# Chunks 1 and 2 of the first layer by seven products per block, in a kernel with a written-out order

## The chip, the cores and the metric

The kernel runs on 1 core of one Trainium2 chip. The metric is the device time of one execution in microseconds (us). The kernel before takes 623.67 us, the median of 3 runs (623.22 to 624.69).

## The reference

Eight batches of 576 tokens with 8 heads of 64 go through a linear attention, and its result through a feed-forward layer whose hidden value is the largest of three products.

```python
q_s = exp(q - max(q, -1)); q_s /= sum(q_s, -1) + 1e-9
k_s = exp(k - max(k, 2));  k_s /= sum(k_s, 2) + 1e-9
x   = q_s @ (k_s^T @ v)                # per batch and head, then 4608 x 512
h   = max(x @ w1, x @ w2, x @ w3)      # w1, w2, w3: 512 x 768
out = h @ w_out                        # 768 x 512, fp32
```

## The kernel before, in words

**Number format.** An operand of the layer is held as two fp32r words, a high one (a cast) and a low one (the value less its cast). A product of two operands is three matmuls, high by low, low by high and high by high. One matmul is 128x128 by 128x512.

**Weights.** The four matrices arrive as pairs of 32-bit words in twelve slices: 0 to 8 are (jp, i), two of the six hidden column blocks of one of w1, w2, w3; 9 to 11 are `w_out`. `Slices.join` rebuilds the fp32 value on VectorE (L535 or ScalarE's L533, then L537, L538, L542); GpSimd adds the low word in two halves (L548, the word sums); ScalarE casts the high word (L556) and VectorE subtracts for the low word (L562, `lo`, whose end is called split). `keep` stores the fp32 value to DRAM (L569). Chunk 0's second product reads `w_out`'s slices 9, 10, 11 in that order of its rows.

**Chunks.** The tokens are nine chunks of 512: rows 0 to 511 of each batch are chunks 0 to 7, and the last 64 rows of all eight batches (the left queries, `left_queries`, L940) are chunk 8. Chunks 0, 1 and 2 are plain: 18 gate groups of 12 matmuls (L1004), the maximum of three (L1017), the split of the hidden value (L1021, L1024), and four second products of 18 matmuls (L1051). A group named (j, i) belongs to block u = 3*(j // 2) + i, so a block is two groups of one chunk. Chunks 3 to 8 are three `Duo`s: two chunks together by Winograd's scheme, per block u of nine seven products P1 to P7 (L1237), six matmuls each, where plain ones would be eight; then seven products for the second layer (L1415). The scheme needs sums of operands: of x (`convert`, L1176 to L1182), of the hidden value (`operands`, L1346 to L1352), and of weights (`mix_weights`, L1086: load, four additions on 128x256 at L1113, a cast, two low words at L1119, store). Its weights are then loaded per product from DRAM (`keep_a`, `keep_s`).

**Attention.** A `Pair` n is two heads of a batch, four pairs to a batch. Batches 0 and 1 (n 0 to 7) have row softmax work in 64 columns; from batch 2 on two pairs share a query tile: load (L660), maximum (L822), 18 exponentials on ScalarE (L826), sums and quotient (L841 to L845), a 32x32 transpose (L850, into `tb`), then small DMAs from `tb` into `qT` (L865), and x by TensorE (L920). The query tile (`qt2`) lies over the slices' staging buffers `wx`. It may be loaded after `clear`: all slices split (`turn`) and those of `wx` stored. There is one such tile, so each load waits for the use before it. Keys from batch 2 on are maximised over partitions by GpSimd (L726); `open_reducer` (L1511) runs that operation once on a dummy first.

**Order.** Each piece of work is a generator of `Step`s (engine, cost, what it waits for). `ORDER`, a list of generator numbers, is written out: word by word it says which generator issues its next step, and a letter behind the number picks the engine where there is a choice. So every engine works in an order fixed in the text, and one engine never passes a step that waits. SyncE issues all data DMAs, in its order too. Costs and ranks in the code made the list; at run time they decide nothing but the fill products (`products_for_nothing`), matmuls put where TensorE was thought idle.

Of the kernel before, what the change touches and what calls it, by code (L numbers as in the profile page):

```python
# [8 lines left out]
F32 = mybir.dt.float32  # L9
# [14 lines left out]

SIGNAL = 0.26
# [32 lines left out]

X_BY_PE = (1, 2, 3, 6)
# [9 lines left out]
2 117 117V 5 124 0 116 3 20 7 124V 117 117 117 124 124 20A 116G 117V 124 27 21 20 20 124V 4 118 118A 27A 28 116 123  # L69
123 116 123 8 130 130 1 116 20 123A 27 9 20 19 137 10 137 131 116 116A 22 131V 27 130 131 6 123 123 12 142 145 138  # L70
130A 119 119 27 27 123A 141 144 144 131 125 125A 119 23V 137 11 29 130 131 130 137A 144 144A 26 126 24 131V 316 130V
317 143 132 144 126 138 132A 138 30V 25 33 126 35 35V 144 126 35 318 133 13 41 133 138 138V 35 137 137 137V 36 145 145
317 316 139 139V 133 144V 35 133 31 35 32 148 43 318 319 319 43A 151 140 318 140 145 145V 34 317 146 151 37 43 43 140
49 140 319 44 151 151A 156 38V 159 43 316 316 149 152 150 334 318 334 43 14 51 51A 42 52 317 146V 320 51 335 320 151
57 151 45 151A 51 59 46V 320 320 59A 155 334 334 162 39 40 65 165 321 51 165 321 321 59 319 335 322 51 50 59 55 334V
322 322 60 67 53 54V 56 73 75 67A 67 165 321 152 152 322 323 323 336 164 59 335 165A 335 157 323 158 158 147 324 324
323 152 81 324 337 324 325 59 325 63 61 152V 67 62V 64 325 325 68 147 67 147 153 165 153A 165 326 336 75A 165A 326 326
67 337 158 326 83 327 327 327 327 75 69 158A 158 159V 47 75 154 76 163 70V 337 75 159 159 159 83A 328 328 71 329 328
48 329 75 77 328 74 329 329 166 79 336 336 97 159V 160 83 78V 83 330 99 158 158V 84 169 83 83 82 154 154 166 166 166
330 330 331 160A 331 335V 85 161 331 330 166V 86V 87 15 72 161 331 161 336V 167 338 99A 99 99 161 339 332 339 332 100  # L80
332 333 333 332 337 99 167V 333 338 338 89 91 168 99 346 314 91A 91 91 103 168 347 101 92 346 91 333 98 168 339 337
338 348 348 348 348 338 349 91 102V 104 93 105 107 108 94V 107V 346 107 346 107 364 347 347 347 365 349 364 349 107
107 109 342 342 349 365 110V 16 18 343 339 339 314 177 343 343 343 178 342 342 314 95 344 344 345 111 341 344 344 345
# [65 lines left out]
""".split()  # L149


# [38 lines left out]
class Streams:  # L190
# [20 lines left out]
    def ready(self, s, engine):  # L211
# [26 lines left out]
        if engine in step.port:  # L238
            t = max(t, self.port)
# [1437 lines left out]
```

## Time and profile before

| | us |
|---|---|
| median of 3 runs | 623.67 |
| profiled execution | 624.85 |
| its span | 623.1 |
| TensorE busy | 612.0 |
| VectorE busy | 447.4 |
| ScalarE busy | 332.5 |
| GpSimd busy | 49.8 |

The profiled execution is 1.75 us longer than its span, and 1.18 us over the median of the runs. The granted clock was 0.999 of full speed. All times of rows are from the start of the span.

### The profile page before, as it was taken

The numbers are of one execution on the slowest core, as the hardware profiler recorded it, in microseconds if no ns is written. First come the engines' busy times: TensorE is split into PE (matmuls) and PEld (weight loads), VectorE is DVE, ScalarE is ACT, GpSimd is POOL, SyncE is SP. The second block draws the span as 40 slices with busy tenths as digits, with TensorE's granted clock in tenths as the row PEclk, the third lists the DMA queues.
The fourth block names the chain that finished last, engine by engine and source line by source line (L and its number), as shares of the span: only waits on it lengthen the run. The fifth ranks groups of instructions, "written<-read, shape, count | busy, mean of one in ns | idle before, by whom it ended". The sixth has DMA issues, their size and how long they took to land.

```text
span 623.1 us, 9728 instructions
## 1 busy us (share of the span) xinstructions
PE 612.0 (98%) x3383; PEld 493.1 (79%) x3383; DVE 447.4 (72%) x668; ACT 332.5 (53%) x847; POOL 49.8 (8%) x44
## 2 busy tenths in 40 slices
PE   6899999999999999999999999999999999999997
PEld 6677778888777777887787878888887788888886
DVE  7999998468877898969476998453778862344573
ACT  5997873366566667763646566232334832223262
POOL 2234333101000100000000000000000000000000
PEclk9999999999999999999999999999999999999999
DMA  8968488589988778988999977687765546666534
GB/s 310 407 245 313 164 259 301 209 309 329 302 301 290 228 246 248 328 308 275 293 315 276 313 202 232 188 250 245 217 199 150 168 140 196 213 209 196 165 99 144
DMA packets 66256, 152.39 MB, mean 245 GB/s; under 512 B 7584, under 2 KB 18464, under 8 KB 62368
## 3 DMA queue, kind: packets, MB, share of 16 engines
q1 hardware_dynamic: 66064, 151.71, 74.4%
q8 instruction: 27, 0.44, 0.3%
q14 instruction: 21, 0.17, 0.1%
q10 hardware_dynamic: 144, 0.07, 0.0%
HBM read 106.92 MB, written 37.75 MB: 232 GB/s over the span
## 4 chain that ended last, share of the span: by engine, by line
PE 96%; DVE 1%; DMA 1%; ACT 1%; issue 0%; SPq 0%; ACTq 0%
PE pf L1237 41%; PE pf L1004 24%; PE pf L1415 14%; PE pf L1051 8%; PE pa L748 3%; PE pa L920 2%; DMA wst<-in_w_dram 1%; PE pa L892 1%; PE sm L773 0%; PE pa L877 0%; PE pa L695 0%; DVE km L671 0%; DVE wx L537 0%; PE pa L977 0%; PE pf L773 0%
## 5 line engine op out<-in xcount | busy, mean ns | idle before, releaser
L1237 PE MATMUL pf<-xb,ws 128*128 128x512 f32 x1134 | 260.3, 390 | 0.0
L1237 PEld LDWEIGHTS pf<-xb,ws 128*128 128x128 f32 x1134 | 212.4, 188 | 44.4
L1004 PE MATMUL pf<-x,wa 128*128 128x512 f32 x648 | 157.6, 397 | 0.0
L1004 PEld LDWEIGHTS pf<-x,wa 128*128 128x128 f32 x648 | 120.0, 188 | 28.1 <-issue 2.1
L1267 DVE TENSOR_TENSOR mm<-pf,mm 128x512 f32<-128x512 f32 x36 | 24.7, 686 | 66.6 <-PE pf L1237 66.6
L826 ACT ACTIVATE qt<-qt,qm 128x64 f32<-128x64 f32 x180 | 60.1, 336 | 10.3 <-DVE rk L755 6.5
L1287 ACT COPY pf<-pf 128x512 f32<-128x512 f32 x27 | 15.5, 575 | 82.4 <-PE pf L1237 73.0
L548 POOL TENSOR_TENSOR wx<-wx,wst 128x512 int32<-128x512 int32 x24 | 34.5, 1458 | 60.1 <-ACT wst L552 21.2
L726 POOL PARTITION_ALL_REDUCE kma<-km x12 | 13.5, 1123 | 313.8 <-DVE km L723 259.9
L1280 ACT COPY u<-pf 128x512 f32<-128x512 f32 x27 | 15.8, 587 | 38.4 <-PE pf L1237 36.2
L826 ACT ACTIVATION_READ_ACCUMULATOR qt<-qt,qm 128x1 f32 x180 | 33.8, 188 | 0.0
L1017 DVE TENSOR_TENSOR m<-pf,m 128x512 f32<-128x512 f32 x36 | 24.4, 684 | 9.7 <-PE pf L1004 8.7
L1051 PE MATMUL pf<-ol,h_h 128*128 128x512 f32 x72 | 28.5, 396 | 0.0
L1113 DVE TENSOR_TENSOR bdf<-bdf 128x256 f32<-128x256 f32 x48 | 20.3, 422 | 11.3 <-DMA bdf<-keep_w 6.4
L1051 PE MATMUL pf<-oh,h_l 128*128 128x512 f32 x72 | 28.1, 390 | 0.0
L1051 PE MATMUL pf<-oh,h_h 128*128 128x512 f32 x72 | 28.0, 389 | 0.0
L1178 DVE TENSOR_TENSOR xb<-xf,xb 128x1024 fp32r<-128x1024 f32 x18 | 21.9, 1221 | 5.5 <-ACT xb L1176 5.4
L1415 PE MATMUL pf<-mix,so 128*128 128x512 f32 x84 | 25.0, 397 | 0.0
L1280 ACT COPY s<-pf 128x512 f32<-128x512 f32 x27 | 15.9, 588 | 14.8 <-PE pf L1237 13.7
L1176 ACT CAST xb<-xf 128x1024 fp32r<-128x1024 f32 x18 | 18.8, 1053 | 8.8 <-DVE xf L1182 6.0
L1352 DVE TENSOR_TENSOR mm<-mm 128x512 f32<-128x512 f32 (+1 forms) x24 | 22.4, 952 | 0.1
L1415 PE MATMUL pf<-op_a,oh 128*128 128x512 f32 x72 | 22.2, 389 | 0.0
(178 smaller groups left out, 912.0 us busy)
## 6 DMA issues: line engine op xcount, KB each, us to landing
ws<-keep_s SPq DMA_DIRECT2D x108, 256.0 KB, 3.8
ws<-keep_a SPq DMA_DIRECT2D x81, 256.0 KB, 3.6
wst<-in_w_dram SPq DMA_DIRECT2D x12, 1024.0 KB, 8.2
keep_a<-wa SPq DMA_DIRECT2D x9, 1024.0 KB, 7.9
keep_s<-mix SPq DMA_DIRECT2D x9, 1024.0 KB, 5.2
vt<-in_v_rows_dram SPq DMA_DIRECT2D x24, 325.0 KB, 5.6
kt<-in_k_rows_dram SPq DMA_DIRECT2D x12, 640.0 KB, 6.1
qt<-in_q_rows_dram SPq DMA_DIRECT2D x12, 576.0 KB, 5.2
```

Source lines behind the costliest of these rows:

```text
L548: nc.gpsimd.tensor_add(out=x.bitcast(I32)[:, at], in0=x.bitcast(I32)[:, at], in1=low.bitcast(I32)[:, at])
L826: nc.scalar.activation(out=rows3[:, s, :], in_=rows3[:, s, :], func=AF.Exp, bias=qm[:, s : s + 1], accum_out=qs[:, s : s + 1],)
L1004: nc.tensor.matmul(out=ps, lhsT=wa[i][:, j, cc, hl], rhs=r, start=(cc == 0 and t == 0), stop=(cc == NC - 1 and t == 2),)
L1017: nc.vector.tensor_max(out=m, in0=self.m.pop((j, i)), in1=m)
L1051: nc.tensor.matmul(out=po, lhsT=l, rhs=r[:, j, :], start=(j == 0 and i == 0), stop=(j == NJ - 1 and i == 2))
L1113: nc.vector.tensor_tensor(out=o, in0=x, in1=y, op=op)
L1178: nc.vector.tensor_tensor(out=xb[i][:, 1], in0=src, in1=xb[i][:, 0].bitcast(F32), op=ALU.subtract)
L1237: nc.tensor.matmul(out=bank[on], lhsT=w[:, k, a], rhs=x[:, b, k], start=(i == 0 and p in ("P1", "P5")), stop=(i == 5), skip_group_check=True,)
L1267: nc.vector.tensor_max(out=m, in0=bank[on], in1=m)
L1280: nc.scalar.copy(out=f, in_=bank[on])
L1352: nc.vector.tensor_tensor(out=o[:, parts[k]], in0=x[:, parts[k]], in1=y[:, parts[k]], op=ALU.subtract)
L1415: nc.tensor.matmul(out=bank[on], lhsT=w, rhs=to[k][b][:, kk - k], start=(kk == 0 and i == 0 and not need), stop=(kk == NK - 1 and i == 2), ...
```

## The change: what it does

1. Chunks 1 and 2 keep eight plain gate groups each, `groups[:8]`, the blocks u = 0 to 3 (`WHOLE = 4`). A new class `First`, a `Duo` for these two chunks, does the blocks u = 4 to 8 by seven products and the second layer by seven products. Its plain weights are read where the slices lie, its mixed weights straight from the mixing's buffers, its x from the plain buffers; `sums` builds four sums of x in weight slots that are done with.
2. The word sums may run on VectorE or GpSimd. In the new order 17 of the 24 are on VectorE and 7 on GpSimd. The steps `lo`, the subtraction of the key maximum, two steps of the query softmax, the mixing's additions and low words have the choice too: of the mixing's 48 additions 18 are on GpSimd, of the twelve `lo` 2.
3. `mix_weights` becomes `mix_loads`, `mix_of`, `mix_store`, `mix_outputs`: two load buffers (`bd2`, `bdf`), `w_out`'s mixes first, then u = 4 to 8, then 0 to 3.
4. `open_reducer` is gone. `keep_weights` goes by jp first. `wa` and `xbuf` are tiles of a third and a quarter of the size. Chunks 1 and 2 leave turned, as the `Duo`s' do (eight turned tiles and one plain for six and three).
5. `ORDER` is new throughout. `w_out`'s slices come in the order 10, 11, 9 (before 10, 9, 11). Chunk 0's 18 groups, the four groups of chunk 1 ahead of the second product, and chunk 0's second product are the same.

```diff
+WHOLE = 4
...
-    for c in range(PAIRED):
-        in_pf += [(c, *g) for g in groups[BEFORE_Y0 if c == 1 else 0 :]]
-        if c == 0:
-            in_pf += [(1, *g) for g in groups[:BEFORE_Y0]]
-        in_pf += [(c, "y", t) for t in range(4)]
+    in_pf += [(0, *g) for g in groups] + [(1, *g) for g in groups[:BEFORE_Y0]]
+    in_pf += [(0, "y", t) for t in range(4)]
+    in_pf += [(1, *g) for g in groups[BEFORE_Y0 : 2 * WHOLE]] + [(2, *g) for g in groups[: 2 * WHOLE]]
+    in_pf += [("S", 1, i) for i in range(4)] + [(1, "y", t) for t in range(6)]
...
             for part in range(2):
-                yield Step("G", 1.3, [("low", n)], gives=("w", n) if part else None, port="G")
+                e = yield Step("GV", (1.3, 0.66), [("low", n)], gives=("w", n) if part else None, port="GV")
                 at = slice(part * CH, (part + 1) * CH)
-                nc.gpsimd.tensor_add(out=x.bitcast(I32)[:, at], in0=x.bitcast(I32)[:, at], in1=low.bitcast(I32)[:, at])
+                xi = x.bitcast(I32)[:, at]
+                unit[e].tensor_tensor(out=xi, in0=xi, in1=low.bitcast(I32)[:, at], op=ALU.add)
...
-            yield Step("G", 1.45, [("ksub", n - 2), "reducer"], gives=("kmt", n))
+            yield Step("G", 1.45, [("ksub", n - 2)], gives=("kmt", n), lib=1)
...
+    MIX_ORDER = [*range(9, 9 + NK), *range(WHOLE, 9), *range(WHOLE)]
+
+    def mix_loads():
+        for n, u in enumerate(MIX_ORDER):
+            j = u - 9
+            after = [("plain", u)] if j < 0 else [("plain", NU + j // 2), ("plain", NU + (j + NK) // 2)]
+            after += [("low_mix", MIX_ORDER[n - 2])] if n > 1 else [("clear", "left")[n]]
+            yield Step("S", 0.55, after, kb=(128, 4096) if j < 0 else (256, 2048), gives=("parts", u))
+            to = (bd2, bdf)[n % 2].rearrange("p n c -> p (n c)")
...
+    def mix_of(n):
...
+            e = yield Step("VG", (0.36, pool(2 * P)), [("parts", u)], port="VG")
+            unit[e].tensor_tensor(out=o, in0=x, in1=y, op=op)
...
+    class First(Duo):
+        def __init__(self, c):
+            super().__init__(c)
+            self.least = WHOLE
+            self.order = [(p, u) for p, u in wino_order if u >= WHOLE]
...
+        def weight_now(self, p, u):
+            kind, r, cc = WINO[p]
+            jp, i = divmod(u, 3)
+            if kind == "a":
+                return wa[i][jp][:, r, 2 * cc : 2 * cc + 2]
+            return mixed_in(u)[r][:, 2 * cc : 2 * cc + 2].bitcast(F32R)
...
+        def sums(self):
...
+            def whole(o, x, k, after, gives):
+                e = yield Step("VG", (dve(2 * CH), 2.1), after, gives=gives, port="VG")
+                unit[e].tensor_tensor(out=o, in0=x[0][k].bitcast(F32), in1=x[1][k].bitcast(F32), op=ALU.add)
+
+            def less(o, x, y, after, gives):
+                e = yield Step("VG", (dve(2 * CH), 2.1), after, gives=gives, port="VG")
+                unit[e].tensor_tensor(out=o, in0=x, in1=y, op=ALU.subtract)
...
-    def open_reducer():
-
-        yield Step("-", 0.0, ["turn", ("h", 0, 2)])
-        yield Step("G", 7.0, gives="reducer", rank=-1000.0)
-        spare = turn_pools[0].tile([P, 1], F32, name="spare")
-        nc.gpsimd.partition_all_reduce(spare, ones, P, bass_isa.ReduceOp.max)
...
+    st.add(first.products(0), GATES_AT)
+    st.add(first.given(), 0.0)
+    st.add(first.all_gates(), 0.0)
+    for g in first.sums():
+        st.add(g, 0.0)
```

## Rows read from the trace of the kernel before

**Rows 1.** The page's part 1: busy time and share of each engine.

```profile
PE 612.0 (98%) x3383; PEld 493.1 (79%) x3383; DVE 447.4 (72%) x668; ACT 332.5 (53%) x847; POOL 49.8 (8%) x44
```

**Rows 2.** Busy time by stretch (columns as in the first line).

```profile
core 0: us, PE busy (x) PEld busy (x) DVE busy (x) ACT busy (x) POOL busy (x), PEclk, DMA share, GB/s
0.00:100.00 100.00, 92.60 (x573) 73.77 (x574) 92.98 (x149) 77.29 (x164) 33.44 (x29) 1.00 0.78 288
100.00:260.00 160.00, 160.00 (x1042) 127.63 (x1041) 124.22 (x207) 96.29 (x343) 13.15 (x12) 1.00 0.83 277
260.00:620.00 360.00, 359.42 (x1771) 291.71 (x1769) 230.21 (x313) 158.84 (x342) 3.19 (x3) 1.00 0.71 220
```

**Rows 3.** The chain of waits in order of time: start, length, what.

```profile
100.98 1.36 PE pf L1051 x6
...
176.64 1.05 PE pa L920 x9
...
258.58 2.72 PE pf L1237 x12
...
387.31 68.00 PE pf L1237 x300
...
619.45 0.58 ACT m L1440
```

**Rows 4.** Timeline of VectorE: start, length, what.

```profile
96.32 2.35 DVE L562 TENSOR_TENSOR ol<-wx,oh 128x1024 fp32r<-128x1024 f32 x2
...
117.61 0.69 DVE L960 TENSOR_TENSOR qt<-qt,qs 128x512 f32<-128x512 f32 x1
...
137.06 1.36 DVE L850 STREAM_TRANSPOSE tb<-qt 128x1152 f32<-128x1152 f32 x1
```

**Rows 5.** Groups of VectorE by shape, 0 to 98.7 us: busy, mean ns, idle before.

```profile
L542 DVE SCALAR_TENSOR_TENSOR wx<-wst,wx 128x1024 uint32<-128x1024 uint32 x11 | 13.4, 1219 | 0.1
L562 DVE TENSOR_TENSOR wa<-wx,wa 128x1024 fp32r<-128x1024 f32 x9 | 12.1, 1343 | 0.2
L537 DVE TENSOR_SCALAR wx<-wx 128x1024 f32<-128x1024 f32 x11 | 10.5, 953 | 1.2 <-ACT wx L533 1.2
L538 DVE TENSOR_SCALAR wx<-wx 128x1024 uint32<-128x1024 uint32 x11 | 7.6, 694 | 0.4
L845 DVE TENSOR_TENSOR qe<-qe,qs 128x512 f32<-128x512 f32 x8 | 5.5, 684 | 0.1
...
L1024 DVE TENSOR_TENSOR h_l<-m,h_h 128x512 fp32r<-128x512 f32 x5 | 4.9, 1003 | 0.0
L841 DVE TENSOR_SCALAR qs<-qs 128x8 f32<-128x8 f32 x8 | 3.4, 426 | 0.2
```

**Rows 6.** Groups of GpSimd by shape, whole span.

```profile
L548 POOL TENSOR_TENSOR wx<-wx,wst 128x512 int32<-128x512 int32 x24 | 34.5, 1458 | 60.1 <-ACT wst L552 21.2 <-DVE wx L542 9.9 <-ACT h_h L1021 6.1
...
L1511 POOL PARTITION_ALL_REDUCE spare<-ones x1 | 0.4, 377 | 7.6 <-issue 7.6
```

**Rows 7.** Timeline of SyncE's queue: query loads, and copies of the transposed queries.

```profile
107.81 0.33 SPq L945 DMA_DIRECT2D qt<-in_q_left_dram  x1
...
121.85 0.34 SPq L660 DMA_DIRECT2D qt<-in_q_rows_dram  x1
...
138.49 0.33 SPq L660 DMA_DIRECT2D qt<-in_q_rows_dram  x1
...
159.77 1.88 SPq L865 DMA_DIRECT2D qT<-tb  x3
```

**Rows 8.** DMA issues, 80 to 165 us: KB each, median us to landing.

```profile
keep_o<-wx SPq DMA_DIRECT2D x3, 512.0 KB, 3.3
...
qT<-tb SPq DMA_DIRECT2D x14, 72.0 KB, 4.9
...
qt<-in_q_left_dram SPq DMA_DIRECT2D x1, 256.0 KB, 4.3
```

**Rows 9.** Groups of VectorE by shape, whole span.

```profile
L1178 DVE TENSOR_TENSOR xb<-xf,xb 128x1024 fp32r<-128x1024 f32 x18 | 21.9, 1221 | 5.5 <-ACT xb L1176 5.4
```

More of the change, by code (lines that the diff above doesn't have):

```diff
@@ L180, with __init__ @@
 class Step:
-    def __init__(self, engine, cost, after=(), gives=None, take=(), free=(), port="", kb=None, rank=None, slack=0.0):
+    def __init__(self, engine, cost, after=(), gives=None, take=(), free=(), port="", kb=None, rank=None, slack=0.0, lib=0):
         self.engine, self.gives, self.take, self.free, self.port, self.kb = engine, gives, take, free, port, kb
         self.cost = cost if isinstance(cost, tuple) else (cost,) * len(engine)
-        self.after, self.rank, self.slack = after, rank, slack
+        self.after, self.rank, self.slack, self.lib = after, rank, slack, lib
 class Streams:
@@ L237, in ready @@
                 t = max(t, f + SIGNAL)
+        if engine == "G" and step.lib != self.lib:
+            t = max(t, self.clock["G"] + RELOAD)
         if engine in step.port:
@@ L286, in issue @@
         self.clock[e] = end
+        if e == "G":
+            self.lib = step.lib
         if e in step.port:
@@ L842, in q_steps @@
             nc.vector.reciprocal(out=qs, in_=qs)
-            which, cost = ("VG", (dve(rows * D), pool(rows * D))) if self.turned else ("V", dve(rows * D))
-            e = yield Step(which, cost, gives=("qn", n), port=which)
+            e = yield Step("VG", (dve(rows * D), pool(rows * D)), gives=("qn", n), port="VG")
             unit[e].tensor_tensor(out=rows3, in0=rows3, in1=qs.unsqueeze(2).broadcast_to([P, rows, D]), op=ALU.mult)
@@ new lines, in mix_store @@
+    def mix_store(u):
+        j = u - 9
+        if j >= 0:
+            yield Step("S", 0.55, [("low_mix", u)], kb=(1024, 1024), gives=("mixed", u))
+            nc.sync.dma_start(
+                out=keep_t[:, :, :, :, j].rearrange("p r c v t n -> p (r c v) (t n)"),
+                in_=mixes[0].rearrange("p r c t n -> p (r c) (t n)"),
+            )
+        elif WHOLE <= u < 9 and (u - WHOLE) % 2:
+            for r in range(2):
+                yield Step("S", 0.5, [("low_mix", u)], kb=(128, 4096), gives=("mixed", u) if r else None)
@@ L1140, in mix_weights, with mix_outputs @@
+    def mix_outputs():
+        after = [*(("mixed", 9 + j) for j in range(NK)), *(("y", 0, t, NJ - 1) for t in range(4))]
+        for hl in range(2):
+            yield Step("S", 0.6, after, gives=("mixed_in", hl), kb=(768, 512))
+            for half in range(2):
+                nc.sync.dma_start(
+                    out=wo[hl][:, 0:NK, (2 * half + 1) * P : (2 * half + 2) * P].bitcast(F32),
+                    in_=keep_t[:, 1, 0, half, :, hl],
                 )
@@ L1164, in convert @@
             if c == PAIRED:
-                before = [[("gates", c - 1), *(("kept", i) for i in range(3))]] * 7
+                y = lambda *names: [("gates", c - 2), "kept", *(("Y", c - 2, p, 1) for p in names)]
+                before = [y("P2"), y("P2"), y("P1"), [*y("P3"), ("out", c - 2, 1, 1, 1)], y("P3"), y("P3", "P4"), y("P4")]
             else:
@@ L1260, in alone @@
             def alone(on, m, after, gives, free):
-                after = [*after, *(old or ()), (gives[0], c, u - 1) if u else None]
+                after = [*after, *(old or ()), (gives[0], c, u - 1) if u > least else None]
                 if i == 0:
@@ L1289, in ago @@
             def ago(what):
-                return (what, c, u - 1) if u else None
+                return (what, c, u - 1) if u > least else None
             def stored(v):
-                return ("out", c - 2, 0, 1, v) if u == 0 and c > PAIRED else None
+                return ("out", c - 2, 0, 1, v) if u == 0 and not least else None
             def met():
@@ L1322, in pieces, with when @@
                 return [[hi[:, 0:1], hi[:, 1:3]], [hi[:, 3:4], op_b]]
-            to = op_c if x == 2 else op_d
-            return [[to[:, t, ks] for ks in (slice(0, 1), slice(1, NK))] for t in range(2)]
+            if x == 2:
+                return [[op_c[:, t, ks] for ks in (slice(0, 1), slice(1, NK))] for t in range(2)]
+            return [[op_dh[:, 0:1], op_dh[:, 1:NK]], op_dl]
+        def when(self):
+            c = self.c
+            top = [[("m", c, 2)], [("m", c, 2), ("m", c, 5)]]
+            end = [[("m", c, 5)], [("m", c, 8)]]
+            free = {
+                0: [("Y", c - 2, "P7", 1)], 1: [("Y", c - 2, "P3", 1)] if c > PAIRED else [("mixed", WHOLE - 1)],
+                2: [("gates", c)], 3: [("gates", c)], 4: [("Y", c, "P1", 1)], 5: [("Y", c, "P5", 1)],
+                6: [("Y", c, "P6", 1)],
+            }
+            return top, end, free
         def operands(self):
@@ L1376, in turned_weights @@
                     yield Step(
-                        "S", 0.4, [("mixed", 8 + NK), ("P2", c, 8)], take=[("so", (c, p, v))], gives=("so", c, p, v),
+                        "S", 0.4, [*(("mixed", 9 + j) for j in range(NK)), *self.room_so[v]], take=[("so", (c, p, v))], gives=("so", c, p, v),
                         kb=(128, 3072),
```

464 lines of the change are left out of this document (317 added, 147 removed), and 91 rows, old and new, of the table ORDER.

## The prediction

> **What bounds the kernel now.** First comes the busy time by engine [rows 1]: TensorE has 98% of the span, VectorE 72%. That is an average, so the second view is by stretch [rows 2]: from 100 us on TensorE is busy in 160.00 of 160 us and then in 359.42 of 360. VectorE has 92.98 of the first 100 us, 124.22 of the next 160, and 230 of the last 360. So there are three regimes: a start in which VectorE is nearly full, a middle with a fifth of VectorE free, and an end where it has room. The third view, the chain in order of time [rows 3], gives the price of a matmul: 300 of them in 68.00 us, 0.2267 each. It also gives three marks. Chunk 0's second product begins at 100.98, x of pair 11 at 176.64, and the first `Duo` (chunk 3) at 258.58. The last mark matters most: every matmul that the change takes away stands ahead of it, and TensorE's work behind it stays as it is. The new time is the old one plus the shift of that mark, if nothing stalls later.
>
> The fourth view is VectorE around the first mark [rows 4]. The low word of `w_out`'s slice 9, which that second product needs, is written at 98.67, and TensorE comes to it at 100.98: a margin of 2.3 us.
>
> **Products.** Gates before: 3 chunks of 18 groups of 12, 648. After: 216 for chunk 0, 2 times 8 groups of 12 = 192, and 5 blocks of 7 products of 6 = 210, together 618. Second products of the plain part: 3 times 72 = 216 before, 72 + 126 = 198 after. So 48 matmuls go, 48 x 0.2267 = 10.9 us [rows 3]. With TensorE still fed, the mark falls from 258.58 to 247.7.
>
> **Word sums, and VectorE up to the first mark.** I counted in both written orders what VectorE must have done before the first second product, each step at its row's duration less 0.06 to 0.08 us by which consecutive ones overlap. Before: 86.8 us. After: 94.7. The new ones are 15 word sums (0.684 each, as the other 512-wide steps with two inputs [rows 5]) and a twelfth slice, since slice 9 now comes last; some steps move behind the mark or to GpSimd. Against these 7.9 us stands what GpSimd took from VectorE. Steps that last 0.694 and 1.219 undisturbed have means of 0.953 (L537) and 1.343 (L562), L1024 has 1.003 for 0.684, and L841's eight small ones take 3.4 us together [rows 5]: 2.8 + 1.1 + 1.6 + about 2 = 7.5 us in 22 sums, 0.34 us per sum. With 15 of them gone from GpSimd that gives back 4 to 5.
>
> The Trainium skill, "SBUF — State Buffer", section "SBUF: two separate sides", says that VectorE and GpSimd share a port pair as an exclusive lock, held for the whole instruction, so that the other engine blocks fully. By that sentence each sum would cost VectorE its whole 1.46 us [rows 6], moving one would gain 0.8, and the first mark would not be late at all. The rows speak against so high a price: VectorE's idle time of the first 100 us is 7.0 in all [rows 2], and its stretched steps make 7.5.
>
> So the last word sum that `clear` waits for, ahead of which 88.9 us of VectorE's steps stand after, comes at 98.67 + (88.9 - 86.8) - 4 = 96.8 (bounds 90 and 101: all 7.5 and 3 us of idle time given back, or nothing and two more), and the second product's operands at 98.67 + 7.9 - 4.5 = 102.1. That alone is a wait of 1.1 us.
>
> **The queries' chain.** Less work stands ahead of x of pair 11: 631 matmuls, not 807. Between the first mark and it are 141 products (32.0 us) and some 6.4 us of small groups, so TensorE would be there at 139.4. But x of pair 11 hangs on one chain through one query tile: last split (3.5 us behind the sum; the stored slice lands after 3.3 [rows 8]), load of queries 8 to their transposes, 121.85 to 138.42, 16.6; left queries, 107.81 to 118.30, 10.5; queries 10, again 16.6 (the row's own 138.49 starts a longer one); eight copies at 1.88 / 3 = 0.63, 5.0; the landing, 4.9 [rows 4, 7, 8]. That is 57.1. I take 55.5, as the left queries' row holds a wait behind chunk 0's outputs on ScalarE; bounds 51 and 62. So x comes at 152.3, and TensorE, which can't pass the step, is 12.9 us late (it waits in part earlier, at pairs 8 to 10 on the same chain). Before, this chain was hidden by 176 more matmuls.
>
> **VectorE between the marks.** Counted as above, 126 us of its steps stand between the first mark and the first `Duo` before, 138 after: `First`'s outcomes, operand sums (1.22 each [rows 9]) and second operands come in, the plain maxima and low words go, and part of the attention moves later. TensorE's work there shrinks from 157.6 to 146.7 us. With the 12.9 us of waits VectorE would be 86% busy where it had 78%, so some steps come late. Bounds: 0 (at 93% in the first 100 us it was still in time at the first mark) and 7 (the stretch as full as the first 100 us, plus one late step per block). I take 2, nearer the first row.
>
> **GpSimd.** `open_reducer` showed 7.6 us of idle time put down to issue ahead of the first partition maximum [rows 6]. In the new order GpSimd changes between partition maxima and plain steps ten times where it was once. Each costs between 0 and 7.6 us of GpSimd; I take 0 on the path, since GpSimd is otherwise idle and keys are needed a batch later. That cover is gone where a mixing's additions stand behind a maximum.
>
> **At nothing.** Mixing loads two at once, `keep_weights`' order, smaller tiles, turned outputs: SyncE's queue issues about the same bytes, and the weight loads of the `Duo`s start no earlier than x. The last store is the same. Ends after the last matmul stay as they are [rows 3].
>
> **Sum.** 624.85 - 10.9 + 12.9 + 2.0 = 628.85 for a profiled execution; the runs' median stands 1.2 under the one before, so 627.6.
>
> **The rivals.**
> *TensorE stays fed* (faster). GpSimd's load on VectorE goes altogether and the start's gaps close, so the sum comes at 90 and, with a chain of 52, x at 142: 2.7 us late, no later wait. 624.85 - 10.9 + 2.7 = 616.7, median 615.5. For it: the gain of matmuls is certain, and 0.34 us per sum is a lower bound if GpSimd's start waits for VectorE too. Against it: slices, chain and 7.9 us more work. 0.27, from 612.6 (nothing late) to 622.
>
> *The port as a full lock* (faster). Fifteen sums of 1.46 us come off VectorE: 21.9 back for 10.3 given, the first mark's operands no later than 92, x at 139 to 143, 612.6 to 616. The Trainium skill's page named above would have it so. The rows bear out a quarter of that price. 0.04.
>
> *GpSimd decides* (slower). Place: a mixed block's additions queued on GpSimd behind a partition maximum, with `First`'s products behind them on TensorE. One change at 7.6 us on the path, on top of the forecast, gives 627.6 + 7.6 = 635.2. It decides from the point where GpSimd's queue is later than the chain of x. For it: 18 of 48 additions there, and ten changes. Against it: 150 us with little work on GpSimd. 0.22, from 631.5 to 638.
>
> *The saving isn't there:* no; the count of matmuls is fixed by the loops.
>
> **How the numbers follow.** 0.2% (1.25 us) is about what a measurement of this kernel can tell from no change, so "same" is 622.4 to 624.9. The forecast's own case has 0.47 and runs from 622 to 631.5: 0.02 of it is faster, 0.10 same, 0.35 slower. With the rivals: faster 0.02 + 0.27 + 0.04 = 0.33, same 0.10, slower 0.35 + 0.22 = 0.57. The likeliest is 627.5. Its own range is 622 to 631.5; for 8 in 10 the range reaches to 616 and to 636, leaving out the fed case's lower part and GpSimd's upper one.
>
> **What would show it.** Right: TensorE has waits between 100 and 155 us, the largest ahead of x of pairs 9 to 11 or the key products, x of pair 11 at 150 to 155, the first `Duo` at 260 to 264, and VectorE over 85% busy in between. The fed case: the first `Duo` below 255 and TensorE without a gap there. GpSimd's case: partition maxima or additions with 7 us of issue ahead of them, and a wait of TensorE that ends on a GpSimd step. The start would speak against my count if TensorE meets the first second product at 101 without waiting. A wait of TensorE behind the first `Duo` would break the premise that the shift of that mark is all.

## The result, and the profile after

The changed kernel takes 633.54 us, the median of 4 runs (630.56 to 635.14). The kernel before, run beside it, took 623.70 (4 runs, 623.22 to 624.69). The ratio is 1.015, with a 95% interval of 1.011 to 1.019: the change costs some 10 us. The runs of 635.14, 633.24, 630.56 and 633.84 us had mean granted clocks of 0.991, 0.994, 1.000 and 0.991; the profile is of the first, in which the clock fell. The profiled execution took 635.14, with a span of 633.4.

Busy time by engine, and by stretch with the same bounds as before [rows 1, 2]:

```profile
PE 610.4 (96%) x3343; PEld 486.3 (77%) x3343; DVE 473.8 (75%) x684; ACT 351.6 (56%) x878; POOL 65.6 (10%) x55
```

```profile
core 0: us, PE busy (x) PEld busy (x) DVE busy (x) ACT busy (x) POOL busy (x), PEclk, DMA share, GB/s
0.00:100.00 100.00, 86.28 (x539) 66.98 (x540) 93.43 (x153) 79.14 (x170) 21.30 (x19) 0.98 0.79 290
100.00:260.00 160.00, 156.40 (x969) 122.28 (x968) 140.62 (x219) 102.56 (x329) 31.63 (x28) 0.98 0.86 287
260.00:620.00 360.00, 358.01 (x1797) 289.45 (x1796) 235.88 (x311) 168.72 (x378) 12.64 (x9) 1.00 0.71 217
```

In the first 100 us TensorE has 6.3 us less busy time than before. In the next 160 us VectorE has 140.62 us of work instead of 124.22, and TensorE, which had no gap there, has one of 3.6 us. The granted clock is 0.98 in both stretches.

The three marks, from TensorE's timeline (start, length, what, and in brackets the idle time ahead and its releaser): first second product, x of pair 11, first `Duo`. The row at 148.20 is TensorE's work just ahead of x of pair 11, and the rows at 177 and 178 us are the place where the clock fell a second time.

```profile
110.38 0.39 PE L1104 MATMUL pf<-ol,h_h 128*128 128x512 f32 x1
...
148.20 3.39 PE L1031 MATMUL pf<-x,wa 128*128 128x512 f32 x12 [0.56 <-DVE mm L1075]
151.53 1.12 PE L947 MATMUL pa<-qT,bd 64*64 64x512 f32 x9
...
176.94 0.49 PE L1329 MATMUL pf<-sum,mix 128*128 128x512 f32 x1 [1.88 <-ACT sum L1629]
178.39 5.06 PE L1329 MATMUL pf<-sum,mix 128*128 128x512 f32 x11 [0.95 <-DVE sum L1633]
...
265.25 1.60 PE L1329 MATMUL pf<-xb,ws 128*128 128x512 f32 x6
```

Against [rows 3], the first mark moved from 100.98 to 110.38, x of pair 11 from 176.64 to 151.53 (176 fewer matmuls stand ahead of it), and the first `Duo` from 258.58 to 265.25. From there to the end of the span it is 368.15 us, where it was 364.7 (623.1 - 258.42; times of this view stand up to 0.17 us ahead of those of the chain in [rows 3]).

What TensorE waited for ahead of the first mark, the larger ones (total, times, longest):

```profile
PE sm L510 <- DMA ident<-in_unit_matrix_dram: 3.9, 1, 3.9
PE pa L723 <- ACT k L705: 3.2, 1, 3.2
PE pf L1031 <- DVE m L1047: 3.1, 1, 3.1
PE pf L801 <- ACT ke L736: 1.5, 1, 1.5
```

All named waits make 13.4 us there; in the kernel before they made 7.4. Both kernels have the same 261 gate products ahead of the mark, 68.0 us of busy time now and 65.4 before. Of these 2.6 us, 1.9 stand in one place: right behind the 3.1 us wait, 15 products took 5.30 us (the granted clock was 0.72 from 82 to 88 us), where 3.4 is usual. So 6.0 us of waits, 2.6 of slower products and 0.9 of products for nothing that the code now issues come to 9.5, about the 9.4 by which the first mark is late.

The chain of queries, on SyncE's queue (start, length, what) [rows 7]: queries 8, the left queries, queries 10, the copies of pair 11.

```profile
101.28 0.33 SPq L688 DMA_DIRECT2D qt<-in_q_rows_dram  x1
...
116.98 0.33 SPq L972 DMA_DIRECT2D qt<-in_q_left_dram  x1
...
127.65 0.33 SPq L688 DMA_DIRECT2D qt<-in_q_rows_dram  x1
...
143.31 5.17 SPq L892 DMA_DIRECT2D qT<-tb  x8
```

And VectorE, with the two last word sums and the last low word of the slices [rows 4]:

```profile
95.95 1.29 DVE L573 CUSTOM_DVE_ANT_0 wx<-wst,wx 128x1024 uint16<-128x1024 uint16 x2 [1.44 <-ACT wst L577]
...
100.00 1.21 DVE L587 TENSOR_TENSOR ol<-wx,oh 128x1024 fp32r<-128x1024 f32 x1
```

The last word sum ends at 97.24, queries 8 are asked for at 101.28, and x of pair 11 comes 54.3 us behind the sum. The last of the eight copies was issued at 147.9 and landed 2.2 us later, at 150.1. TensorE, busy since 148.20, came to x of pair 11 at 151.53, so here its own work and not the chain set that mark, by 1.4 us. At x of pair 9 it was the other way: the last copy landed at 139.9, x had begun at 138.88, and its products took 2.3 us where those of pair 11 took 1.1.

### The profile page after: what moved, and what is told of

The parts are those of the page before. It is cut to its first block, busy times and chain, and to the rows that moved or that the text cites. A ratio compares the mean times of both kernels' runs of the same rounds, so it can differ in the third digit from the quotient of the medians.

```text
span 633.4 us, 9769 instructions
## 1 busy us (share of the span) xinstructions
PE 610.4 (96%) x3343; PEld 486.3 (77%) x3343; DVE 473.8 (75%) x684; ACT 351.6 (56%) x878; POOL 65.6 (10%) x55
## 4 chain that ended last, share of the span: by engine, by line
PE 55%; DVE 11%; DMA 6%; issue 2%; SPq 1%; ACT 1%; DVEq 0%; ACTq 0%
PE pf L1329 39%; PE pf L1517 14%; DMA ws<-keep_a 3%; DMA bd<-keep_w 1%; DMA keep_s<-mix 1%; PE pa L947 1%; DVE sumf L1621 1%; DVE qt L872 1%; DVE op L1450 1%; PE pa L776 1%; DVE mix L1183 1%; DVE mm L1454 1%; DMA qt<-in_q_rows_dram 1%; SPq L892 1%; DVE mm L1372 1%
## 5 line engine op out<-in xcount | busy, mean ns | idle before, releaser
L1031 PE MATMUL pf<-x,wa 128*128 128x512 f32 x408 | 103.2, 405 | 4.1 <-DVE m L1047 3.1
L1031 PEld LDWEIGHTS pf<-x,wa 128*128 128x128 f32 x408 | 76.2, 191 | 25.3 <-DVE m L1047 3.5
L1363 DVE TENSOR_TENSOR mm<-pf,mm 128x512 f32<-128x512 f32 x44 | 30.1, 687 | 73.6 <-PE pf L1329 73.4
L1454 DVE TENSOR_TENSOR mm<-mm 128x512 f32<-128x512 f32 (+1 forms) x32 | 31.2, 980 | 0.3
L1329 PE MATMUL pf<-sum,mix 128*128 128x512 f32 x54 | 16.5, 448 | 2.8 <-ACT sum L1629 1.9
L1517 PEld LDWEIGHTS pf<-mix,so 128*128 128x128 f32 x84 | 15.8, 188 | 3.7
L1542 ACT COPY m<-pf 128x512 f32<-128x512 f32 x16 | 9.4, 586 | 16.4 <-PE pf L1517 16.4
L1369 DVE TENSOR_TENSOR u<-pf,u 128x512 f32<-128x512 f32 x18 | 12.4, 690 | 8.0 <-PE pf L1329 7.9
L761 ACT ACTIVATE kt<-kt 128x1280 f32<-128x1280 f32 x12 | 15.2, 1276 | 5.7 <-DVE kt L756 5.6
L1517 PEld LDWEIGHTS pf<-op_a,oh 128*128 128x128 f32 x84 | 15.7, 188 | 3.3
```

Source lines behind the costliest of these rows:

```text
L761: nc.scalar.activation(out=kt, in_=kt, func=AF.Exp)
L1031: nc.tensor.matmul(out=ps, lhsT=wa[i][j // 2][:, j % 2, cc, hl], rhs=r, start=(cc == 0 and t == 0), stop=(cc == NC - 1 and t == 2),)
L1329: nc.tensor.matmul(out=bank[on], lhsT=w[:, k, a], rhs=self.operand(p, b, k), start=(i == 0 and p in ("P1", "P5")), stop=(i == 5), skip_gro ...
L1363: nc.vector.tensor_max(out=m, in0=bank[on], in1=m)
L1454: nc.vector.tensor_tensor(out=o[:, parts[k]], in0=x[:, parts[k]], in1=y[:, parts[k]], op=ALU.subtract)
L1517: nc.tensor.matmul(out=bank[on], lhsT=w, rhs=to[k][b][:, kk - k], start=(kk == 0 and i == 0 and not need), stop=(kk == NK - 1 and i == 2), ...
```

## The experiments

All kernels are variants of the changed kernel unless said otherwise, so each stands against its 633.54 us. Runs of the kernel before beside them had medians of 624.08 to 624.47. The changed kernel was not run again beside them, and its own runs spread from 630.56 to 635.14, so medians that differ by some 2 us are not told apart by the time alone. The places move with the execution too: eight kernels whose order is the same up to there have the last word sum at 96.19 to 98.94. Distances between places are the safer numbers. Line numbers of variants differ by a few from those above. Where a mark is given without a row, it is read from the same timelines. The places in one table, in us:

| kernel | last word sum ends | first second product | x of pair 11 | behind the sum | first `Duo` | median |
|---|---|---|---|---|---|---|
| changed | 97.24 | 110.38 | 151.53 | 54.3 | 265.25 | 633.54 |
| old_start | 104.39 | 100.94 | 157.75 | 53.4 | 270.62 | 640.67 |
| sums_gpsimd | 99.87 | 111.05 | 153.42 | 53.6 | 266.10 | 637.14 |
| fewer_products | 98.67 | 111.81 | 150.40 | 51.7 | 263.42 | 632.39 |
| keep_clock | 103.42 | 116.51 | 157.27 | 53.9 | 272.69 | 641.24 |
| clock_short | 100.17 | 113.27 | 153.81 | 53.6 | 266.51 | 634.44 |
| sums_first | 97.14 | 110.20 | 152.60 | 55.5 | 272.43 | 640.89 |
| two_sums | 96.19 | 109.25 | 150.59 | 54.4 | 261.93 | 631.44 |
| weights_first | 98.91 | 111.97 | 152.88 | 54.0 | 265.50 | 632.00 |
| own_tile | 98.94 | 111.98 | 156.47 | 57.5 | 269.89 | 637.30 |
| own_and_sums | 97.34 | 110.39 | 154.87 | 57.5 | 275.66 | 643.98 |
| all_three | 98.46 | 111.54 | 157.26 | 58.8 | 267.98 | 635.38 |

**old_start: which of the two is the clock of this stretch, TensorE or the chain?** The written order of the kernel before is used up to the first second product, the changed one behind it.

```diff
-ORDER, words up to chunk 0's first second product: as in the changed kernel
+ORDER, words up to chunk 0's first second product: as in the kernel before
 (the other words in the order of the changed kernel)
```

> The written order up to chunk 0's first second product is that of the kernel before (all word sums on GpSimd, slice 11 last), behind it that of the changed kernel. If the queries' chain sets x of pair 11 (our theory): the first second product is back at 101 us, but the last split falls to about 107 from 101, so x of pair 11 comes at 157 for 151.5, the first Duo at 270 or so, and the time is 636 to 641. If the changed kernel loses its time in the start (rival: 9.4 us up to the first second product): the time falls to 623 to 626.

Measured: 640.67 us (639.16 to 641.31), ratio to the kernel before 1.0257 [1.0241, 1.0274]. The timeline, with the two marks of TensorE and GpSimd's last word sums between them:

```profile
100.94 0.39 PE L1102 MATMUL pf<-ol,h_h 128*128 128x512 f32 x1
...
101.62 2.77 POOL L571 TENSOR_TENSOR wx<-wx,wst 128x512 int32<-128x512 int32 x2 [6.36 <-DVE wx L564]
...
157.75 1.12 PE L945 MATMUL pa<-qT,bd 64*64 64x512 f32 x9
```

The start is repaired, the first second product comes 9.4 us sooner, and x of pair 11 comes 6.2 us later, with a last word sum that ends 7.2 us later. The last copy of its queries landed at 156.5, so x could not have come before that, however early TensorE began. But TensorE was not standing ready for it either. Behind its repaired start it had 11.4 us of named waits (4.8 for VectorE's low word of the hidden value, 3.8 for ScalarE's keys, 2.8 for GpSimd's low word of a slice), and its granted clock was 0.50 from 108 to 126 us. So the run shows that an earlier start is worth nothing while the sum is late; it doesn't separate the chain from these waits.

**fewer_products: the same question from the other side.** 24 of chunk 0's second products are left out.

```diff
-            for i, (l, r) in enumerate(((hh, wo[1]), (hh, wo[0]), (hl, wo[0]))):
+            for i, (l, r) in enumerate(((hh, wo[0]), (hl, wo[0]))):
```

> The changed kernel without the 24 matmuls of chunk 0's second product that take the hidden value's high word by w_out's low word (those rows of the output lose that part). They stand between the first second product and x of pair 11. If the queries' chain sets x of pair 11 (our theory), it stays at 151 to 152 us and the time falls by 0 to 2 us, to 631.5 to 633.5. If TensorE's own work sets it (rival), 24 x 0.2267 = 5.4 us go, to 628.

Measured: 632.39 us (632.07 to 634.73), 1.0136 [1.0116, 1.0156]. Of the 5.4 us of products left out, 1.15 reach the median, which is less than the runs' spread; behind the sum, x of pair 11 comes 2.6 us sooner (51.7 for 54.3). TensorE's waits from 100 to 160 us, the three largest of 3.6 in all:

```profile
PE pa L776 <- DMA vt<-in_v_rows_dram: 1.2, 1, 1.2
PE pa L947 <- DMA qT<-tb: 1.0, 1, 1.0
PE pa L947 <- DVE km L751: 0.6, 1, 0.6
```

With less to do, TensorE stands before the products of x of pair 9 (L947), for the copies of the turned queries and for VectorE. The changed kernel itself shows only 0.6 us of named waits in this stretch: its TensorE came late enough, by the 9.4 us of the start, to find the queries almost ready.

The 2.6 us have a place. The chain itself passes through TensorE, which must turn the left queries before their tile is free for queries 10. In the changed kernel, VectorE's last step on them and TensorE's:

```profile
123.64 0.69 DVE L987 TENSOR_TENSOR qt<-qt,qs 128x512 f32<-128x512 f32 x1
...
126.93 0.65 PE L992 MATMUL pa<-ident,qt 128*128 128x128 f32 x4
```

They were ready at 124.33, and TensorE, which takes its work in the written order, came to them 2.6 us later. In fewer_products they were ready at 125.23 and turned at 125.47. So the chain with TensorE in time takes at most 51.7 us, and the 54.3 of the changed kernel hold TensorE's lateness.

**sums_gpsimd: the price of a word sum on GpSimd.** All 24 sums go there, where 7 were.

```diff
-ORDER: 17 words of the sums end in V
+ORDER: these words without V (GpSimd)
```

> The changed kernel with all 24 word sums on GpSimd. Our price (0.61 us of VectorE's time per sum moved to it, 0.34 us of stretching per sum on GpSimd): 17 sums give VectorE 10.4 - 5.8 = 4.6 us back, the last split and x of pair 11 come 3 to 5 us earlier, the time is 629 to 631. Rival, the full lock (1.46 us per sum on GpSimd): 24.8 - 10.4 = 14 us more, 640 to 648.

Measured: 637.14 us (635.26 to 637.8), 1.0208 [1.0191, 1.0225]. Both expectations missed, the truth lies between them. VectorE sheds 17 sums of 0.61 us, 10.4 in all, and yet the last sum ends 2.6 us later: by this estimate a sum costs VectorE (10.4 + 2.6) / 17, about 0.77 us, while it runs elsewhere (the 2.6 is no larger than the spread of that place between executions). How that happens is seen in the timeline at 41 us, GpSimd first, then VectorE:

```profile
41.28 3.04 POOL L571 TENSOR_TENSOR wx<-wx,wst 128x512 int32<-128x512 int32 x2
...
42.42 0.73 DVE L559 TENSOR_SCALAR wx<-wx 128x1024 f32<-128x1024 f32 x1 [0.74 <-ACT wx L555]
43.18 1.69 DVE L560 TENSOR_SCALAR wx<-wx 128x1024 uint32<-128x1024 uint32 x1
```

GpSimd's second sum ends at 44.32. VectorE's step, 0.69 us when undisturbed, ends at 44.87, 0.55 behind it: it did next to nothing until GpSimd was done.

**keep_clock: what does the fall of the clock cost?** Products for nothing fill the waits at 79 and 177 us.

```diff
+            if at == 342:
+                self.spare(28)
...
+                    if least and u == least and p == "P1" and i == 5:
+                        for _ in range(30):
+                            nc.tensor.matmul(
+                                out=bank[on][:, 0:P], lhsT=ident, rhs=zero.broadcast_to([P, P]), start=False, stop=False,
+                                skip_group_check=True,
+                            )
```

> The changed kernel with 28 and 30 small products for nothing put into TensorE's two longest waits, at 79 and 175 us, behind which its granted clock fell. If the fall of the clock is a cost of its own: the clock stays at 1.00 in 80 to 90 and 176 to 190 us. Of the 1.9 us (15 matmuls in 5.30) and 2.6 us (11 in 5.06) that the slow clock took, the chain theory leaves the second alone: 630.5 to 631.5; without that chain both come back: 629. If the clock costs nothing that the wait had not cost: 633.5.

Measured: 641.24 us (639.77 to 642.13), 1.0268 [1.025, 1.0285]. The clock stayed at full in both places, but a filler, a plain f32 product on 128 columns, takes 0.229 us, as long as a useful one on 512 (fp32r), so that the fillers took 6.4 and 6.9 us, twice the waits. The run says nothing about the price.

**clock_short:** the same with 13 products at each place.

> 13 products for nothing (0.229 us each, 3.0 us) at each of the two places where the granted clock falls, at 79 us and at 177 us, so that they end about when the waits of 3.1 and 2.8 us end. Theory (the slow clock behind a wait is a cost of its own, about 2.6 us at each place, of which the queries' chain hides most of the first): the granted clock stays at 1.0, the stretch from x of pair 11 to the first Duo shrinks by 2 to 3 us and the time is 630.5 to 631.5 us. Rival (the wait alone costs, the slow clock lies where TensorE has to wait anyhow): 633 to 634.5 us.

Measured: 634.44 us (633.98 to 636.57), 1.017 [1.0145, 1.0196]. TensorE's timeline at the second place:

```profile
177.95 3.06 PE L1333 MATMUL pf<-zero,ident 128*128 128x128 f32 x26
...
181.63 2.90 PE L1337 MATMUL pf<-sum,mix 128*128 128x512 f32 x11 [0.15 <-DVE sum L1641]
```

The 26 records are 13 products. The next products run at full speed, 11 of them in 2.90 us instead of 5.06, and x of pair 11 to the first `Duo` takes 112.7 us instead of 113.7. So 2.2 us of slow clock were taken away there and 1.0 came out; TensorE then waits for VectorE in small pieces. The time is the rival's: by fillers nothing is gained.

**sums_first: is the wait at 177 us a matter of order?** The operand sums of `First` go ahead of one step of the queries and of a mixing's step on VectorE, and GpSimd's two go to VectorE.

```diff
-ORDER: ... 625G ... 627G ... (among steps of the queries and of the mixing)
+ORDER: ... 625V ... 627V ... (ahead of them)
```

> The same instructions as the changed kernel, but VectorE makes the operand sums of the first block products of chunk 1 ahead of one step of the queries and of one mixing step, and two of those sums move from GpSimd to VectorE. Theory (the 5.4 us between x of pair 11 and the first Duo's product come from TensorE waiting 2.8 us for these sums and then running at half clock for about 2.6 us): both go, the stretch x of pair 11 to first Duo shrinks from 113.7 to 108.5 to 110 us, and the time is 628 to 630 us. Rival (VectorE is the bound of this whole stretch, so that work put back there stalls TensorE later): the stretch stays at 112 to 114 us and the time at 632 to 635 us.

Measured: 640.89 us (640.07 to 643.02), 1.0273 [1.0246, 1.03]. TensorE's timeline:

```profile
182.99 1.57 PE L1327 MATMUL pf<-sum,mix 128*128 128x512 f32 x6
190.48 2.93 PE L1327 MATMUL pf<-x,wa 128*128 128x512 f32 x6 [5.92 <-DVE mm L1361]
```

The wait at 177 us falls to 0.7 us, and one of 5.92 at 184.6 us, on a maximum of VectorE, takes its place: the rival's mechanism, at a higher price than it named. In this order the steps put ahead cost more on another; no other order was tried.

**two_sums: or is it GpSimd that holds VectorE?** Only the two sums change engine, nothing changes its place.

```diff
-ORDER: ... 625G ... 627G ...
+ORDER: ... 625V ... 627V ...
```

> The changed kernel with the two operand sums that GpSimd makes for the first block products of chunk 1 (128x1024 each, at 161 and about 167 us) on VectorE instead, in the same order. Theory (while GpSimd works on such a sum VectorE stands, its 1.22 us sum took 3.43 us beside one of 2.73 us; on VectorE each sum takes 1.22 us, so it is about 1 us a sum to the good): the waits at 176.9 and 178.4 us shrink by 1 to 2 us, x of pair 11 to the first Duo falls from 113.7 to 111.5 to 113 us, and the time is 631.5 to 633 us. Rival (GpSimd's work lies beside VectorE's as the word sums' did in the kernel before, at a fraction of its time): VectorE has 2.4 us more to do, the waits grow and the time is 635 to 637 us.

Measured: 631.44 us (630.66 to 633.38), 1.0119 [1.01, 1.0138]. In the timeline of the changed kernel, GpSimd's sum and VectorE's step beside it:

```profile
160.79 2.73 POOL L1625 TENSOR_TENSOR sumf<-sumf 128x1024 f32<-128x1024 f32 x1 [3.46 <-DVE sumf L1621]
...
161.18 3.43 DVE L1621 TENSOR_TENSOR sumf<-x,x 128x1024 f32<-128x1024 f32 x1
...
164.53 1.87 DVE L1075 TENSOR_TENSOR mm<-pf,mm 128x512 f32<-128x512 f32 x3
...
164.73 2.42 POOL L1625 TENSOR_TENSOR sumf<-sumf,sumf 128x1024 f32<-128x1024 f32 x1 [1.21 <-issue]
```

GpSimd's ends at 163.52 and VectorE's, begun at 161.18, at 164.61: 1.1 us behind it, about its own 1.22. Not every step is held: the three at 164.53, which read one input from PSUM (`pf`), took 1.87 us beside GpSimd's next sum, and in two_sums, where no GpSimd step runs beside them, 1.88. With both sums on VectorE the step at 161.18 takes 1.22, the waits fall from 2.8 to 2.1 us, and the clock, at 0.50 (1.2 of 2.4 GHz) in the changed kernel from 178 to 184 us, stays at 1.00. TensorE's timeline:

```profile
175.24 0.50 PE L1327 MATMUL pf<-sum,mix 128*128 128x512 f32 x1 [1.19 <-ACT sum L1627]
176.69 2.91 PE L1327 MATMUL pf<-sum,mix 128*128 128x512 f32 x11 [0.95 <-DVE sum L1631]
```

From x of pair 11 to the first `Duo` it is 111.3 us, 2.4 less. The theory's direction held, and time and stretch came out just below its ranges. The waits shrank by 0.7 us, where it had 1 to 2; most of the gain is the clock, with eleven products in 2.91 us for 5.06. Six profiled kernels with the old order of this stretch, the changed one among them, take 112.6 to 113.7 us for it, with 4.1 to 5.1 for the eleven products; the two with both sums on VectorE in this order take 111.3 and 110.7 (all_three), with 2.91. So the edit is worth 1.3 to 2.4 us of this stretch; the 2.1 us between the medians alone would not show it.

**before_fewer: the first term alone.** The kernel before, with 48 products of chunk 2's gates left out.

```diff
                 for t, (hl, r) in enumerate(((1, h), (0, lo), (0, h))):
+                    if c == 2 and t == 1 and i:
+                        continue
```

> The kernel before, with 48 of the 216 gate products of chunk 2 left out (one of three in 12 of its 18 blocks), and nothing else changed: the first term of the sum by itself, without new sums, order or word sums. Theory (TensorE bounds all of this stretch, each product left out is worth its 0.2267 us): 624.1 - 10.9 = 613.2 us, 612.5 to 614.5. Rival (the queries' chain or VectorE stand just behind TensorE there already in the kernel before, and give back what TensorE saves): 616 to 622 us.

Measured: 618.05 us (617.18 to 619.09) against 624.47, ratio 0.9895 [0.9878, 0.9911]: 6.4 us, not 10.9. The first `Duo` begins at 252.45. TensorE's waits from 112 to 262 us, where the kernel before had none:

```profile
PE pf L1053 <- ACT h_h L1023: 1.2, 1, 1.2
PE pf L1053 <- DVE m L1019: 1.1, 1, 1.1
PE pa L920 <- DVE qs L841: 0.4, 1, 0.4
```

Of the 4.9 us that this mark falls short, 2.7 show as these waits; where the other 2.2 went isn't settled. The kernel before was balanced: what TensorE saved, VectorE and ScalarE gave back in part.

**weights_first: the wait behind the first Duo.** Four copies of turned queries go one by one behind the next weight loads on SyncE's queue.

```diff
-ORDER, SyncE's words: ... 379 379 253 379 379 266 379 379 250 250 250 250 ...
+ORDER, SyncE's words: ... 379 250 379 250 253 379 250 379 250 266 379 379 ...
```

> The changed kernel with the four copies of turned queries that stand on the SP queue at 302 us ahead of the streamed weights' load set one by one behind the next four weight loads. Theory (the waits for streamed weights behind the first Duo, 1.4 + 0.3 us, come from loads issued late behind these copies): they go, first Duo to the end falls from 368.2 to about 366.5 us and the time to 631.5 to 632.5 us. Rival (the weights land late because the DMA engines are 0.9 busy there, whatever the order): the waits stay and the time is 633 to 635 us.

Measured: 632.0 us (630.18 to 633.07), 1.012 [1.0102, 1.0138]. In the changed kernel SyncE issues, and TensorE waits (total, times, longest):

```profile
301.82 0.32 SPq L1296 DMA_DIRECT2D ws<-keep_s  x1
302.19 3.67 SPq L892 DMA_DIRECT2D qT<-tb  x4
305.99 0.51 SPq L1296 DMA_DIRECT2D ws<-keep_a  x1
```

```profile
PE pf L1329 <- DMA ws<-keep_a: 1.7, 2, 1.4
```

With the copies spread out the wait is 0.5, and from the first `Duo` to the end of the span it takes 365.8 us instead of 368.15. So the order of this queue can make the wait. How much of the 2.4 us it is worth isn't settled: nine variants that keep the old order of these loads take 366.0 to 367.5 us there, with waits for streamed weights of 0.4 to 1.7, so the changed kernel's profile was a long one.

**own_tile, own_and_sums, all_three: can the chain be shortened?** The left queries get the free half of another tile, so that the load of queries 10 need not wait for them. own_and_sums adds sums_first; all_three adds two_sums and weights_first, with the left queries' steps left in their place. The diff shows the start of the code change; `ORDER` changes with it.

```diff
-        yield Step("S", 0.5, ["clear"], take=[("qt", "left")], gives=("q", "left"), kb=(128, 2048))
-        ql = qt2.rearrange("p m s d -> p (m s) d")[:, 0:H, :]
+        yield Step("S", 0.5, ["clear"], take=[("qT", "left")], gives=("q", "left"), kb=(128, 2048))
+        qT2 = turn_pools[0].tile([P, 2, S], F32, name="qT", bufs=1)
+        ql = qT2[:, 1, :CH].rearrange("p (h d) -> p h d", h=H)
```

> The left queries of batches 0 to 3 get a place of their own (the free half of the transposed queries' tile), so that the load of pair 10 and 11's queries no longer waits for them and can start some 10 us sooner; the steps on the way are put into an order that allows it. Theory (x of pair 11 hangs on the one tile of queries): it no longer comes at 151.5 us but when TensorE's own work is done, 110.4 + 38.4 = 148.8 us, and the time falls by 2 to 3 us to 630.5 to 632 us. Rival (TensorE's own work and its late start set the mark, the queries are only just behind): x of pair 11 moves by under 1 us and the time is 633 to 634 us.

> Both edits at once, the left queries' own place and the sums ahead. Theory (two terms of the sum, one ahead of x of pair 11 and one behind it): the gains add up to 6.5 to 8 us, and the time is 625.5 to 627 us. Rival (they are one delay, which the slower of the two sets): the time is that of the better of the two alone, within 1 us.

> The changed kernel with three edits: the two operand sums on VectorE (2.1 us to the good by itself), the four copies behind the weight loads (1.5 us by itself), and the left queries in a place of their own with their steps left where they were, only the load of pair 10 and 11's queries sent ahead, straight behind the transposes of pair 8 and 9. Theory (three terms at three places, and x of pair 11 hangs on the one tile of queries): x of pair 11 comes at the mark + 38.4 to 39.5 us instead of + 41.2, and the time is 633.5 - 2.1 - 1.5 - 2.4 = 627.5 us, 626.5 to 628.5. Rival (TensorE's own work sets x of pair 11, the tile of queries costs nothing): 629.3 to 631 us. Neither is faster than the kernel before.

Measured: own_tile 637.3 us (634.13 to 639.29), 1.0205 [1.0169, 1.0241]; own_and_sums 643.98 (643.22 to 644.43), 1.0315 [1.0299, 1.0332]; all_three 635.38 (633.67 to 636.69), 1.0178 [1.0163, 1.0193]. All three missed. The load of queries 10 did go out sooner, at 119.17 us in all_three instead of 127.65. But the timeline of all_three, ScalarE and then TensorE, shows what came in its place:

```profile
144.84 0.58 ACT L1006 COPY left<-pa 128x512 f32<-128x512 f32 x1 [8.22 <-DMA out_dram<-left]
...
145.48 0.36 PE L945 MATMUL pa<-qT,bd 64*64 64x64 f32 x1 [4.33 <-ACT left L1006]
```

The copy on ScalarE that frees a PSUM bank for x of pair 9 waits for chunk 0's outputs to be stored, and I had put these behind eight copies on SyncE's queue. After this wait the clock was at 0.60 from 146 to 152 us. In own_tile TensorE waited 2.46 us for the left queries themselves. Whether the tile alone, with an order that suits it, gives the 2.4 us stays open. The other two terms held in all_three: 110.7 us from x of pair 11 to the first `Duo`, 365.7 from there to the end of the span. two_sums and weights_first together would give 633.5 - 2.1 - 1.5 = 629.9 if their medians add (an estimate, not run). No variant that does all the work was faster than the kernel before.

## Why the prediction was right, and where its sizes were off

The sign was right, and the reason in the main: TensorE's saving is given back ahead of x of pair 11, under which the chain of queries stands as a floor. The time was 6 us over the forecast's 627.6. It lies 2 us above the range of the forecast's own case (622 to 631.5) and inside the one for 8 in 10 (616 to 636). On the profiled span the sum and the measurement stand so:

| term | predicted | measured |
|---|---|---|
| 48 matmuls fewer | -10.9 | -10.9 in work (only -6.4 when tried alone) |
| x of pair 11 late | +12.9 | +12.1 (151.53 - 139.4), 9.4 of it in the start |
| between x of pair 11 and the first `Duo` | +2.0 | +5.4 (113.7 where the forecast has 108.3 and the 2.0) |
| behind the first `Duo` | 0 | +3.5 (1.3 to 2.8 in nine variants) |
| sum | +4.0 | +10.1 (span: 633.4 - 623.1 = 10.3) |

"So x comes at 152.3": it came at 151.53. Its parts held too. The last word sum was forecast at 96.8 and ended at 97.24; the second product's operands at 102.1, and the last low word ended at 101.21; the chain at 55.5 us, and x came 54.3 behind the sum. Nine kernels that leave the query tile alone, the changed one among them, have 51.7 to 55.5 us. In all of them but old_start the first mark also follows the sum, at 11 to 13 us, so that only old_start, and fewer_products with less work behind that mark, tell the two apart.

That this term fits to 0.8 us is in part luck. It was forecast as a wait of TensorE for the chain, with 1.1 us of waiting ahead of the first mark. In the changed kernel TensorE lost 9.4 us ahead of that mark and 2.7 behind it (41.15 us to x of pair 11 for a forecast 38.4), and it came to x 1.4 us after the last copy had landed. Without TensorE's late start the chain would have put x at 97.24 + 51.7 = 148.9 at the latest (an estimate, with the chain as fewer_products has it), 9.5 us late. So the chain by itself accounts for most of the term, and the late start adds some 2.6 us.

Of the signs named ahead of the result, x of pair 11 at 150 to 155 us and VectorE over 85% busy came true. The waits of TensorE between 100 and 155 us came to 0.6 us and some 1.2 inside x of pair 9, and the first `Duo` came at 265.25, not at 260 to 264.

Where TensorE would wait was wrong. "It waits in part earlier, at pairs 8 to 10": it waited, and ran slow, for most of those us before 88, on ScalarE's key steps and on a late maximum of VectorE. I counted how much VectorE must have done by the first mark, and that count held, but not in which order: 93.43 of 100 us busy leave no room for a step that TensorE needs early and that stands late in line. This cost less than its 9.4 us, since the chain would have held TensorE anyway (fewer_products: of 5.4 us saved, 2.6 arrive at x of pair 11).

"I take 2" for VectorE between the marks is the first mis-sized term. It measured 5.4 (4.3 to 5.4 in the six profiles with this order): waits of 1.9 and 1.0 us for `First`'s operand sums, and about 2.6 for eleven products at half clock behind them. VectorE has 88% of the stretch from the first mark to the first `Duo` (136.95 of 154.87 us), as forecast with over 85%. What I left out was GpSimd: two of the sums run there and hold VectorE, 1.3 to 2.4 us of the stretch (two_sums). That another order only moved the wait (sums_first) fits VectorE as the bound here, but one order doesn't show it.

The premise "the new time is the old one plus the shift of that mark, if nothing stalls later" failed at its condition, the second mis-sized term. 2.0 of the 3.5 us are waits of TensorE, 1.7 for streamed weights; "SyncE's queue issues about the same bytes" was beside the point, as the queue's order can make such a wait (weights_first). Some 0.7 is work that now stands behind the mark (40 small key products more and 3 large ones fewer), the rest isn't named by a row.

"With TensorE still fed, the mark falls to 247.7" was never to be had: alone the saving brought it to 252.45 (before_fewer). An engine that is busy in 160.00 of 160 us says that the others are in time, not by how much.

Rivals. *TensorE stays fed* needed the last sum at 90 and x at 142; they came at 97.24 and 151.53. *GpSimd decides* gave an interval that holds the time, by another way than it said: no wait of TensorE in the changed kernel ends on a GpSimd step. The pauses ahead of partition maxima and plain steps are there (7.39 and 8.10 us put down to issue, at 259.85 and 296.30), off the path. *The port as a full lock* was too quickly put aside. The mean of 0.34 us per sum [rows 5, 6] is a mean over steps that were held and steps that were not. Row by row, the VectorE steps at 43.18 and 161.18, which met a running GpSimd step, did next to nothing until that one ended, and those at 164.53 ran on beside it. Full blocking is what the Trainium skill says in "SBUF — State Buffer", section "SBUF: two separate sides", of VectorE's steps with two SBUF inputs or in a two-port mode (a condition that the forecast left out), and the row at 161.18, a step with two inputs, agrees; the one at 43.18 has a single input, and no row shows its mode. So the lock's price fits the two steps shown that were held. What it makes of the time depends on how many are: some 0.8 us per sum in sums_gpsimd, and a kernel 1.5% slower, not faster.

## What to carry to other kernels

Where one engine is busy all the time, try what its saving is worth before counting on it: leave some of its work out, and see which engine steps in (here 6.4 of 10.9 us were to be had). Follow a new order by its longest chain through a single buffer, from the step that starts it; TensorE's own work is only one of the chains. Where a term fits in size, compare when the awaited copy landed with when it was used: two late paths that meet look like one. Count an engine's steps by the order in which others need them, not by their total, and look row by row at VectorE beside GpSimd: a mean hides steps that stood still.

## What I had not expected of the hardware

The granted clock fell to its lower level (0.50 from 178 to 184 us) behind short waits and stayed there for some us when the work came back: 15 products in 5.30 us behind a wait of 3.1, 11 in 5.06 behind 1.9 and 1.0 with little in between, but 11 in 2.91 behind 1.2 and 1.0 in two_sums. In those two profiles a wait shorter by 0.7 us went with eleven products shorter by 2.2. Executions of one kernel differ in this as well: the changed kernel's mean clocks were 0.991 to 1.000, and the run at 1.000 was its shortest.

A filler, a plain f32 product on 128 columns, took 0.229 us, as much as a useful product on 512.

One SyncE copy of 72 KB usually takes 0.63 us to issue [rows 7]; the four at 302 us took 3.67, 0.92 each, so that a place in the queue can cost more than its count says.
